# The first batch by pieces of two token tiles, all scores on eight 64 by 32 tiles, and TensorE in program order

**Chip, cores, metric.** One core of one Trainium2 chip. The metric is the device time of one execution in microseconds (us), median over runs. The kernel before takes 174.58 us (174.41 to 174.96, 3 runs).

## The reference

Attention over 4 batches, 8 heads, 768 tokens, head size 64, with a local window of 96 keys, 8 global keys and a distance bias; its output goes through a layer that multiplies by sines and cosines of a projection, mixes tokens with two 768 by 768 matrices, and applies a channel matrix.

```python
scores = scale * q @ k^T + bias            # bias = -slope[head] * distance
scores = where(is_global | is_local, scores, -1e9)
x = (softmax(scores) @ v) as [batch, token, 512]
theta = x @ w_theta
y = w_tok_r @ (x * cos(theta)) + w_tok_i @ (x * sin(theta))
u = x + y
out = u + max(u @ w_ch, 0)
```

## The kernel before

It works in stages that overlap between batches: *scores* and exponentials, *values*, transposes of x (xT), *theta* (projection, sines, products), *mix* (the token matrices, 72 matmuls of 512 columns a batch), transposes of u (uT), *chan* (the channel matrix), store. A head part, in program order, does the attention of batch 1. From then on the mixes of one batch ("main") are woven with the attention of the next ("side"), and a scheduler may reorder each engine.

The scores need the keys of tile jt and, for the next query tile, the last 96 of them with the 8 global keys in front. The kernel keeps a copy of the keys for that (kG):

```python
def kglob(b, p):
    kG = ...                                   # [128, 4, 128]
    nc.vector.tensor_copy(out=kG, in_=kT[:, T:5*T] ...)
    nc.vector.tensor_copy(out=kG[:, :, 0:NG], in_=kT[:, None, 0:NG] ...)

def score_mms(b, p, c):                        # one chunk: two key tiles, two heads
    for j in range(2):
        jt = 2 * c + j
        for part in range(2 if jt + 1 < NT else 1):
            for hh in range(2):
                R = slice(D * hh, D * (hh + 1))
                lhsT = kG[R, jt - 1, :] if part and jt else kT[R, own]
                nc.tensor.matmul(pb[:, hh, o:o + T], lhsT=lhsT, rhs=qT[R, (own, nxt)[part]], ...)

# preparation of a head pair: VectorE copies (qkn), TensorE transposes, copies qT (VectorE), kT (ScalarE)
# (cut) the weave of batch 1's main part; load_all_v(2) is its first side step
side[:0] = [(0, lambda: load_all_v(2))]        # fill of a column of ones on VectorE, then a DMA from GpSimd
weave(main, side, 0.3 if b == 0 else 0.0, 0.9)
```

The softmax here doesn't subtract the row's maximum and nothing guards it: scores larger than these inputs give would overflow.

## Time and profile before

| | before |
|---|---|
| time | 174.58 us |
| span of the profiled run | 172.6 us |
| TensorE / VectorE / ScalarE busy | 159.9 / 128.5 / 99.1 us |
| score matmuls, key copies | 352, 32 |
| instruction fetches for TensorE (queue q8) | 11 |

How to read: in the lines of profiles PE is TensorE, PEld its weight loads, DVE VectorE, ACT ScalarE, POOL GpSimd and SPq SyncE's queue; L12 is line 12 of that kernel's own source. Busy time of TensorE joins overlapping matmuls, so 93% busy isn't a full engine. The most useful ruler here turned out to be another one: the start of the n-th mix weight load, which is the same piece of work in every variant. Before, the 24th stands at 40.0 us, the first of batch 2 at 80.0, of batch 3 at 113.7, of batch 4 at 147.6, and the last of these loads (of 288) at 165.5.

### The profile page before, as it was taken

Reading aid. Unit: us, or ns where it says so; the run is one execution under the profiler, and the core shown is the slowest. Engines: PE = TensorE matmul, PEld = TensorE weight load, DVE = VectorE, ACT = ScalarE, POOL = GpSimd, SP = SyncE. Lnnn points to the kernel's source line nnn. Section 1 sums busy time; section 2 is a strip of 40 time slices with the busy share of each in tenths; the row PEclk is TensorE's granted clock in tenths of the full one; section 3 lists DMA queues with packets and bytes.
Section 4 is the critical chain, followed back from the end, with each engine's and each line's share of the span. In section 5 each row is a group of like instructions: output and inputs, shape, how many; then the busy total and the mean of one; then the engine's idle time right before and its main releaser. Section 6 shows DMA issues by size and latency. Waiting matters only on the chain.

```text
span 172.6 us, 3652 instructions
## 1 busy us (share of the span) xinstructions
PE 159.9 (93%) x1482; PEld 83.5 (48%) x1482; DVE 128.5 (74%) x288; ACT 99.1 (57%) x124; POOL 37.9 (22%) x45
## 2 busy tenths in 40 slices
PE   6479979999999999999999998999999989999991
PEld 1245655455756566544455463444554634444440
DVE  7678965678999999999587588597786837724443
ACT  2479676999497595489834740979348308500010
POOL 8974355005272010099300000000000000000000
PEclk9999999999999999999999999999999999999998
DMA  5999999999999999879999997787138571323335
GB/s 146 192 193 178 210 208 209 204 204 171 160 204 175 166 155 128 132 97 154 210 141 80 224 158 165 138 152 226 30 76 113 135 171 40 142 41 102 100 93 182
DMA packets 75088, 25.92 MB, mean 150 GB/s; under 512 B 63168, under 2 KB 72128, under 8 KB 75072
## 3 DMA queue, kind: packets, MB, share of 16 engines
q0 software_dynamic: 45680, 12.45, 78.4%
q1 hardware_dynamic: 28976, 12.72, 36.6%
q10 hardware_dynamic: 416, 0.52, 0.9%
q8 instruction: 11, 0.18, 0.4%
q14 instruction: 5, 0.04, 0.1%
HBM read 25.69 MB, written 6.29 MB: 185 GB/s over the span
## 4 chain that ended last, share of the span: by engine, by line
PE 59%; DVE 21%; ACT 10%; DMA 6%; issue 1%; SPq 0%; DVEq 0%; ACTq 0%
PE ps L409 29%; PE ps L434 10%; PE pb L389 5%; PE pb L295 4%; PE pb L352 4%; DVE x_sb L362 4%; ACT etab L142 3%; PE ps L389 3%; ACT e L302 3%; DMA qk<-in_k_dram 3%; DVE kG L218 2%; DVE e L312 2%; ACT cs L395 2%; DMA kT<-qk 2%; DMA xT<-x_sb 2%; PE ps L244 2%
## 5 line engine op out<-in xcount | busy, mean ns | idle before, releaser
L409 PE MATMUL ps<-zri,w_tokT 128*128 128x512 bf16 x288 | 70.6, 380 | 0.3 <-DVE o_sb L440 0.2
L302 ACT ACTIVATE e<-pb 128x1024 bf16<-128x1024 f32 (+1 forms) x48 | 43.6, 958 | 23.1 <-PE pb L295 22.9
L409 PEld LDWEIGHTS <-w_tokT 128*128 128x128 bf16 x288 | 26.1, 98 | 29.0 <-issue 1.0
L414 DVE TENSOR_TENSOR u<-x_sb,ps 128x512 bf16<-128x512 bf16 x24 | 16.4, 682 | 14.6 <-PE ps L409 14.6
L434 PE MATMUL ps<-w_ch_bf,uT 128*128 128x512 bf16 x96 | 24.2, 379 | 0.0
L398 DVE TENSOR_TENSOR zri<-x_sb,cs 128x512 bf16<-128x512 bf16 x48 | 17.9, 418 | 8.0 <-ACT cs L395 7.8
L440 DVE SCALAR_TENSOR_TENSOR o_sb<-ps,u 128x512 f32<-128x512 f32 (+1 forms) x25 | 16.5, 662 | 3.1 <-PE ps L434 3.1
L395 ACT ACTIVATE cs<-pb,halfpi 128x1024 bf16<-128x1024 f32 x8 | 8.9, 1116 | 15.7 <-PE pb L389 15.7
L312 DVE TENSOR_TENSOR e<-e,etab 128x1024 bf16<-128x1024 bf16 (+1 forms) x24 | 14.7, 615 | 3.4 <-ACT e L302 3.4
L389 PE MATMUL pb<-w_theta_bf,xT 128*128 128x512 bf16 x64 | 15.2, 379 | 1.0 <-DMA xT<-x_sb 1.0
L295 PE MATMUL pb<-qT,kT 64*128 64x128 bf16 x224 | 15.6, 219 | 0.6 <-DVE qT L211 0.3
L295 PEld LDWEIGHTS <-kT 64*128 64x128 bf16 x224 | 9.0, 94 | 14.1 <-issue 12.5
L389 PEld LDWEIGHTS <-xT 128*128 128x128 bf16 x96 | 9.0, 98 | 12.0 <-DMA xT<-x_sb 2.4
L428 ACT COPY uT<-ps 128x512 bf16<-128x512 bf16 x7 | 4.1, 587 | 18.6 <-PE ps L427 18.6
L352 PEld LDWEIGHTS <-e 128*128 128x128 bf16 x352 | 12.7, 97 | 3.3 <-issue 1.5
L434 PEld LDWEIGHTS <-uT 128*128 128x128 bf16 x96 | 8.9, 98 | 10.0 <-ACT uT L428 0.3
L295 PE MATMUL pb<-qT,kG 64*128 64x128 bf16 x128 | 11.7, 217 | 1.2 <-DVE kG L220 1.2
L88 POOL DMA_DIRECT2D vn<-in_v_dram x5 | 9.7, 1930 | 12.2 <-DVE vn L68 10.6
L362 DVE TENSOR_TENSOR x_sb<-pb,rec 128x768 bf16<-128x768 f32 x12 | 11.4, 949 | 0.3
L315 DVE TENSOR_TENSOR e<-e,etab 128x1024 bf16<-128x1024 bf16 x12 | 8.2, 684 | 2.8 <-ACT e L302 2.8
L352 PE MATMUL pb<-vn,e 128*128 128x65 bf16 x168 | 9.6, 193 | 0.3 <-DVE x_sb L362 0.3
L82 POOL DMA_DIRECT2D qk<-in_q_dram x8 | 7.4, 920 | 8.8 <-DVE qkn L229 5.0
(74 smaller groups left out, 203.0 us busy)
## 6 DMA issues: line engine op xcount, KB each, us to landing
out_dram<-o_sb SPq DMA_DIRECT2D x23, 256.0 KB, 2.4
vn<-in_v_dram POOLq DMA_DIRECT2D x3, 768.0 KB, 22.7
qk<-in_q_dram POOLq DMA_DIRECT2D x2, 768.0 KB, 21.0
qk<-in_k_dram POOLq DMA_DIRECT2D x2, 768.0 KB, 23.6
w_nat<-in_moe_w_tok_r_dram POOLq DMA_DIRECT2D x3, 384.0 KB, 13.7
w_nat<-in_moe_w_tok_i_dram POOLq DMA_DIRECT2D x3, 384.0 KB, 14.6
vn<-in_v_dram POOLq DMA_DIRECT2D x2, 384.0 KB, 8.9
qk<-in_q_dram POOLq DMA_DIRECT2D x8, 96.0 KB, 9.7
```

The source lines that it names most:

```text
L295: nc.tensor.matmul(pb[:, hh, o:o + T], lhsT=lhsT, rhs=qT[R, (own, nxt)[part]], start=bool(b), stop=bool(b) or (jt == NT - 1 or (j == 1 and ...
L302: ins = nc.scalar.activation(e_c, pb[:, :, 0:n], AF.Exp, scale=scale).ins
L312: nc.vector.tensor_mul(e_c, e_c, tab[:, :, s0:s0 + n // T].rearrange("p a s n -> p a (s n)"))
L352: nc.tensor.matmul(o, lhsT=l_, rhs=r_, start=(i_ == 0), stop=(i_ == len(mms) - 1))
L362: nc.vector.tensor_mul(xv, po4[:, :, :, 0:D], rec.to_broadcast([T, n, NT, D]))
L389: nc.tensor.matmul(pb[j_] if last else pb[:, j_, :], lhsT=xT[:, dc, st(j_)], rhs=w_theta_bf[:, dc, :], start=(dc == 0), stop=(dc == NC - 1))
L395: nc.scalar.activation(o, p_, AF.Sin, **bias)
L398: nc.vector.tensor_mul(zri[b][:, i_, 2 * c + j_, :].rearrange("p (g d) -> p g d", g=NP), xb[:, :, 2 * c + j_, :], cs[:, i_, j_].rearrange( ...
L409: anchor["pe"] = nc.tensor.matmul(ps, lhsT=w_tokT[wi][:, st, tt * T:(tt + 1) * T], rhs=zri[b][:, wi, st, :], start=(st == 0 and wi == 0), ...
L414: anchor["dve"] = nc.vector.tensor_add(u_sb[b, tt].rearrange("p (g d) -> p g d", g=NP), x_sb[b][:, :, tt, :], ps.rearrange("p (g d) -> p g ...
L434: nc.tensor.matmul(ps_c, lhsT=uT[:, dc, :], rhs=w_ch_bf[:, dc, :], start=(dc == 0), stop=(dc == NC - 1))
L440: nc.vector.scalar_tensor_tensor(o_sb[:, cols], in0=ps_c[:, cols], scalar=0.0, in1=u[:, cols], op0=ALU.max, op1=ALU.add)
```

## The change

Its intent: no key copies on VectorE (a group of 32 keys is its own TensorE tile, so the global keys can take the place of the first group), an earlier start of theta in batch 1, and a TensorE order that puts two chunks into each visit to the small tiles. The weave of batch 1 starts at 0.1 instead of 0.3. The diff, cut to its core:

```diff
-    def kglob(b, p): ...                       # and all its calls
     def score_mms(b, p, c):
-            for part in range(2 if jt + 1 < NT else 1):
-                for hh in range(2):
-                    lhsT = kG[R, jt - 1, :] if part and jt else kT[R, own]
-                    nc.tensor.matmul(pb[:, hh, o:o + T], lhsT=lhsT, rhs=qT[R, (own, nxt)[part]], ...)
+            for g in range(T // GS):           # four groups of 32 keys
+                own, P = slice(jt * T + g * GS, jt * T + (g + 1) * GS), slice(g * GS, (g + 1) * GS)
+                parts = [(own, 0, 1), (slice(0, GS), 1, n)][:n] if g == 0 and jt else [(own, 0, n)]
+                for keys, a, z in parts:
+                    for hh in range(2):
+                        nc.tensor.matmul(pb[P, hh, ...], lhsT=kT[R, keys], rhs=qT[R, ...], ...)
 # head: values0 and xtrans0 by chunks of two token tiles; theta, its products and the
 # first 24 mixes follow chunk by chunk (cut, about 150 lines)
+    ordered.enter_context(tc.manual_schedule(engines={PE}))     # until the end of the last weave
-        weave(main, side, 0.3 if b == 0 else 0.0, 0.9)
+        weave(main, side, 0.1 if b == 0 else 0.0, 0.9)
```

## The prediction

> **What bounds the kernel now.** I read the page's busy line first, then a table of busy time by stretch (columns: stretch, its length, then busy time and instruction count of each engine, granted clock, DMA), then the chain of waits, then the groups, and last the single matmuls of one stretch of scores.
>
> ```profile
> PE 159.9 (93%) x1482; PEld 83.5 (48%) x1482; DVE 128.5 (74%) x288; ACT 99.1 (57%) x124; POOL 37.9 (22%) x45
> ...
> 16.00:28.00 12.00, 10.19 (x171) 6.72 (x170) 10.12 (x29) 9.52 (x12) 6.07 (x6) 1.00 1.18 209
> 28.00:37.00 9.00, 8.90 (x52) 4.15 (x50) 5.81 (x16) 7.43 (x10) 0.41 (x1) 1.00 1.26 205
> ...
> 44.00:56.00 12.00, 11.79 (x148) 7.17 (x145) 12.00 (x28) 8.71 (x11) 5.38 (x7) 1.00 2.02 182
> 56.00:72.00 16.00, 15.28 (x201) 9.55 (x200) 16.00 (x36) 9.50 (x13) 1.18 (x2) 1.00 2.16 150
> ```
>
> TensorE is 93% busy, but busy time joins overlapping matmuls, their latency included, so it hides slack. I counted it otherwise: from start to start, a 512-column matmul takes 0.216 us, a 128-column one 0.056, a 65-column one 0.030, and a pair of score matmuls 0.056. Summed over the matmuls of a stretch this gives the work; the rest is slack. All matmuls come to 145.4 us. Slack by stretch: 0 to 28 us 11.9; 28 to 44 us 0.9; 44 to 72 us 5.0; 72 to 141 us 5.3; after that 4.2, mostly the last store. So two places can give: the head, and the stretch at 44 to 72 us, where VectorE is busy all of the time and sets the pace.
>
> The chain of waits (start, length, what) says the same:
>
> ```profile
> 0.74 4.37 DMA qk<-in_k_dram
> ...
> 7.78 1.01 DVE kG L218
> 8.81 0.18 DVE kG L220
> 9.04 0.25 PE pb L295 x2
> 9.32 1.94 ACT e L302 x2
> ...
> 36.01 1.28 ACT L142
> 37.31 5.12 ACT etab L142 x8
> 42.43 0.47 ACT uT L428
> 42.90 0.70 ACT kT L251
> 43.62 0.29 DVE kG L218
> ```
>
> The key copy kG stands before the first exponential; at 36 to 42.4 us the table load and the eight bias tables on ScalarE hold up the preparation of the second batch; then VectorE leads until 61 us; from there TensorE leads.
>
> **What the Trainium skill says.** (1) "TensorEngine Tiling (Array Packing)", section Key Properties: tiles work independently, but a change of tiling mode drains TensorE. The trace agrees with the drain: between the last 512-column matmul and the first score there are 0.31 us of start-to-start time where 0.22 would do, and on the way back 0.15 where 0.06 would do; a visit to the score mode costs some 0.19 us. (2) "TensorE: Matmul & The Clock Gate", section Measured speedup vs the span model: packed tiles start some 4 ns apart, for row and column tiles alike. For two row tiles the trace agrees: two score matmuls of 0.216 us are over within 0.22. No run yet shows column tiles. (3) The tiling page, section Restrictions: column tiling turns off the fast weight load. A load of 128 columns shows as 94 ns here and hides behind matmuls; what a load of 32 columns costs, the trace does not show.
>
> ```profile
> 81.50 0.22 PE L295 MATMUL pb<-qT,kG 64*128 64x128 bf16 x2
> 81.55 0.22 PE L295 MATMUL pb<-qT,kT 64*128 64x128 bf16 x2
> 81.61 0.22 PE L295 MATMUL pb<-qT,kG 64*128 64x128 bf16 x2
> 81.66 0.22 PE L295 MATMUL pb<-qT,kT 64*128 64x128 bf16 x2
> 81.72 0.22 PE L295 MATMUL pb<-qT,kG 64*128 64x128 bf16 x2
> 81.87 1.25 PE L409 MATMUL ps<-zri,w_tokT 128*128 128x512 bf16 x5
> ```
>
> **Part 1, scores on 64 by 32 tiles.** Before, a pair of heads took 22 score matmuls, 352 in all. Now chunks of two key tiles take 18, 20 and 18, so 56 a pair of heads and 896 in all: TensorE goes from 1482 to 1482 + 544 - 1 (one warm-up less) = 2025. The columns that each tile streams are the same: 256 a key tile, two matmuls at 0.056 = 0.112 us before, one of 256 (estimated 0.109 from 256/512 of 0.216) now. With eight tiles at 4 ns each, TensorE breaks even in steady flow. But matmuls start in order: in the first group of 32 keys the global keys need a second load and a second matmul, and groups 2 to 4 wait behind it, so a visit ends about 0.06 + 0.02 us later than before: 0.08 x 18 to 24 visits = +1.4 to +1.9 us, most of it in the TensorE-led part. In return the program order puts two chunks in every visit. The table by stretch shows visits split before: 54 changes of mode after 44 us, where 18 undivided visits make 36. (54 - 36) x 0.095 = -1.7 us. The two cancel.
>
> **Part 2, no key copies.** These groups go altogether:
>
> ```profile
> L218 DVE COPY kG<-kT 128x512 bf16<-128x512 bf16 x16 | 6.2, 388 | 1.3 <-DMA kT<-qk 0.7 <-ACT kT L211 0.5
> L220 DVE COPY kG<-kT 128x32 bf16<-128x32 bf16 x16 | 2.9, 179 | 0.2
> ```
>
> That is 9.1 us of VectorE. It counts only where VectorE leads: 1.2 us ahead of the first exponential, and about 2.2 us (four pairs at some 0.55) between 43 and 51 us. After 72 us it is hidden behind TensorE.
>
> **Part 3, the head in pieces.** New VectorE work: 12 divisions of 256 columns in place of 8 of 384 (estimate 12 x 0.54 against 8 x 0.68, +1.0), two copies taken over from ScalarE (+1.2). Net VectorE about -6.5, so near 122 us busy and 265 instructions. The dates: inputs land at 5.1 as before; cast 5.2 to 6.1, transposes to 6.6, copies to 7.5, scores to 8.0, so the first exponential is at 8.0 instead of 9.3. Then it slows: heads 2 and 3 land only at 8.3 to 8.9 (issue at 1.35 and 2.18 plus 7 us), so their cast cannot come forward. From there on TensorE, in order, costs about 1.0 us a chunk (bias 0.43, visit 0.19, scores 0.3) plus turns and values, 14 to 15 us for the rest; ScalarE's own sum is 8 x 0.93 + 4 x 0.72 + 3 x 0.70 = 12.4. The last exponential then ends at about 23.5 instead of 25.3, and theta starts at about 23.5 instead of 28.0. Not all of these 4.5 us is won: 1.7 us of values and transposes and 0.7 of weight transposes now come later, and in the strict order VectorE (24 to 37 us: divisions, copies, four products of 0.4 us each of three chunks) makes the first mixes wait some 2 us. By hand I arrive at 24 mix matmuls at 39 us, where the kernel before has 20 and one weight tile more. Gain on TensorE: 0 to 1.5 us. But ScalarE ends its sines some 2 us earlier, so the bias tables end near 40.5 and the second batch's preparation starts earlier.
>
> **Part 4, TensorE in program order.** No cost of its own; it removes the scheduler's filling of gaps. I allow 0 to +2 us.
>
> **Sum.** Head -0.8; 40 to 72 us: VectorE 2.2 us lighter and started 2 us earlier, limited by the 5.0 us of slack of which drains keep about 2.5: -2.3; after 72 us -0.3 (merged visits, no key copy in the chain at 106 us, against the 0.08 a visit); stalls of the fixed order +0.7. Together -2.7 from 174.58: **171.8 us**.
>
> **Rivals.** (a) The weight loads of 32 columns do not overlap. At some 27 ns each (an estimate: a 65-column matmul with its load is spaced 30 ns in the trace), 20 loads are 0.54 us a chunk instead of 0.22: +0.3 x 36 chunks where TensorE leads = +11 us, so 183 to 185. For it: the skill's word on fast load. Against: row tiles overlap down to 3 or 4 ns in the trace. (b) The fixed order stalls: scores wait for a free buffer, and TensorE, which before went to other work, stands still. Chunk pairs come some 2 us apart and two exponentials take 1.94, so it is tight; 18 pairs at 0.2 us = +3.6, so 176. (c) The head gains fully: if the divisions and products flow without the 2 us wait, mixes start near 30 us and the whole lead of 3 to 4.5 us stays: 168 to 169.
>
> **Range and chances.** The middle case is 171.8; (b) and a part of (a) give the upper end, 175.8, and (c) the lower, 168.5. The border for faster is 171.1, just below my middle. Faster 0.36, within 2% 0.54, slower 0.10 (that is (a)).
>
> **What would show it.** Matmuls 2025; kG gone; score matmuls of eight tiles starting within some 30 ns; a two-chunk visit at 0.6 to 0.7 us; first exponential near 8.0; last near 23.5; first sine near 25.5; bias tables ending near 40.5; VectorE near 122 us. Wrong would be: score spacing near 27 ns a matmul; waits of TensorE of over 0.2 us before scores in the later batches; or a dense TensorE from 24 us on, with no wait for the products.

## More of the kernel before

In batches 2 to 4 the transposes of x, u and some q and k are DMAs issued from SyncE, which also issues the stores: one queue, in order.

One line of the profile that the prediction did not look at will matter, TensorE's instruction fetches among the DMA queues (packets, MB, share):

```profile
q8 instruction: 11, 0.18, 0.4%
```

## The result, and the profile after

The changed kernel takes **183.06 us** median (181.22 to 184.04, 4 runs); before, in the same rounds, 174.77. The ratio is 1.0425 (95% interval 1.0324 to 1.0526): slower. A ratio is the mean time of one kernel's fast runs over that of the other's fast runs of the same rounds, so not quite the ratio of the medians. The profiled run is one marked slow (184.04 us, over 1.5% above the fastest); its mean TensorE clock, 0.991, lies between those of the runs marked fast (0.986, 0.987, 0.999). So what is read from it alone counts for that run only; the long copy and the theta stages below show in fast profiles of variants too (e1, e7).

The page of the changed kernel (busy times; then the span in 40 slices; then TensorE's fetches; then the scores):

```profile
PE 160.2 (88%) x1996; PEld 86.1 (47%) x2025; DVE 126.7 (70%) x265; ACT 97.6 (54%) x119; POOL 38.2 (21%) x45
...
PEclk9999999999699999999999999999999999999999
...
q8 instruction: 16, 0.26, 0.7%
...
L286 PE MATMUL pb<-qT,kT 64*32 64x256 bf16 (+1 forms) x896 | 17.4, 257 | 5.1 <-ACT e L294 2.3
```

The counts are as predicted (2025 weight loads; 29 matmul records are missing). TensorE has no more to do, yet the span is 9.4 us longer. The clock is down in one slice, at 45 to 50 us. And there are 16 fetches instead of 11.

A visit of two chunks to the small tiles, from the sequence of TensorE's work in batch 2:

```profile
87.30 0.38 PE L423 MATMUL ps<-zri,w_tokT 128*128 128x512 bf16 x1
87.61 0.63 PE L286 MATMUL pb<-qT,kT 64*32 64x256 bf16 x38
88.17 0.39 PE L423 MATMUL ps<-zri,w_tokT 128*128 128x512 bf16 x1
```

38 matmuls in 0.56 us from the first to the next mix; the same visit before took 0.55. The eight tiles of a group start 3.3 ns apart, and a load of 64 by 32 lasts 88 to 93 ns and hides. So the tiles themselves are what the prediction said.

Where the time went, by the start of the n-th mix weight load (us). The last two columns are the *theta stages*, from the last mix of one batch to the first of the next, which wait for the last xT:

| kernel | 24th | first of batch 2 | of 3 | of 4 | last | stage before 3 | stage before 4 |
|---|---|---|---|---|---|---|---|
| before | 40.0 | 80.0 | 113.7 | 147.6 | 165.5 | 8.7 | 8.6 |
| changed | 38.8 | 86.3 | 121.2 | 157.0 | 174.9 | 9.7 | 9.8 |

The head is 1.2 us ahead. The next 48 mixes, beside batch 2's attention, lose 7.5 us. The two theta stages lose 1.0 and 1.2. The mixes of batches 2 and 3 lose 0.2 and 0.7, those of batch 4 nothing.

The waits of the first loss, in the changed kernel's timeline (start, length, engine, work, idle time before and releaser):

```profile
41.14 0.10 DVE L68 MEMSET vn<- 128x48 bf16 x1
...
42.09 2.27 POOL L88 DMA_DIRECT2D vn<-in_v_dram  x1 [13.44 <-DVE qkn L221]
42.16 2.62 DVE L221 COPY qkn<-qk 128x768 bf16<-128x768 bf16 x3 [0.74 <-DMA qk<-in_k_dram]
...
44.71 0.94 DVE L241 COPY qT<-ps 128x768 bf16<-128x768 bf16 x1
...
45.70 0.49 PE L168 MATMUL ps<-ident,w_nat 128*128 128x128 bf16 x6 [1.95 <-DVE qT L241]
```

and the same in the kernel before, from the timelines of GpSimd and of VectorE:

```profile
39.05 2.21 POOL L88 DMA_DIRECT2D vn<-in_v_dram  x1 [10.64 <-DVE vn L68]
```

```profile
41.28 1.16 DVE L229 COPY qkn<-qk 128x768 bf16<-128x768 bf16 x4
42.35 0.95 DVE L249 COPY qT<-ps 128x768 bf16<-128x768 bf16 x1
```

Before, the fill of ones came at 38.1 us, so GpSimd issued the V load from 39.05 to 41.26 and the four copies of q and k ran undisturbed, 0.35 us each. After, the fill comes at 41.1, and GpSimd issues from 42.09 to 44.36. The new head makes it late: with the old weave start it still comes at 40.4 (e2 and h2 below). What the early weave start does is to bring the copies onto the issue; in e2 and h2 they begin at 44.4 and 44.2, after it. Here, of the three copies beside it, one lasts 2.08 us (42.44 to 44.52). It ends 0.16 us after the issue; in the fast profiles of e1, e7 and h1 a copy of 2.1 us ends 0.15 to 0.17 us after it. The Trainium skill, "SBUF — State Buffer", section Who interferes with whom, says that VectorE and GpSimd share a pair of ports under an exclusive lock, that a VectorE copy can take it, and that whichever comes second blocks fully. This trace agrees. The copy holds up qT, and TensorE, in its fixed order, stands at 43.7 to 45.7 us.

### The profile page after: what moved, and what is told of

The parts are those of the page before. It is cut to its first block, busy times and chain, and to the rows that moved or that the text cites.

```text
span 182.0 us, 4682 instructions
## 1 busy us (share of the span) xinstructions
PE 160.2 (88%) x1996; PEld 86.1 (47%) x2025; DVE 126.7 (70%) x265; ACT 97.6 (54%) x119; POOL 38.2 (21%) x45
## 4 chain that ended last, share of the span: by engine, by line
PE 56%; DMA 21%; ACT 10%; POOL 5%; DVE 4%; issue 3%; DVEq 0%; POOLq 0%
PE ps L423 27%; DMA qk<-in_k_dram 11%; PE ps L448 10%; DMA w_nat<-in_moe_w_tok_r_dram 7%; ACT e L294 5%; PE pb L392 4%; PE pb L341 4%; PE pb L286 4%; DMA xT<-x_sb 3%; PE ps L236 2%; POOL qk L73 2%; PE ps L392 2%; POOL vn L88 2%; DVE qkn L221 2%; ACT cs L400 1%
## 5 line engine op out<-in xcount | busy, mean ns | idle before, releaser
L423 PE MATMUL ps<-zri,w_tokT 128*128 128x512 bf16 x269 | 66.6, 382 | 2.9 <-issue 1.5
L448 PE MATMUL ps<-w_ch_bf,uT 128*128 128x512 bf16 x91 | 23.3, 379 | 0.4 <-issue 0.2
L286 PE MATMUL pb<-qT,kT 64*32 64x256 bf16 (+1 forms) x896 | 17.4, 257 | 5.1 <-ACT e L294 2.3
L400 ACT ACTIVATE cs<-pb,halfpi 128x1024 bf16<-128x1024 f32 x9 | 10.0, 1116 | 21.3 <-PE pb L392 20.5
L392 PE MATMUL pb<-w_theta_bf,xT 128*128 128x512 bf16 x70 | 17.1, 380 | 3.1 <-DMA xT<-x_sb 3.0
L286 PEld LDWEIGHTS <-kT 64*32 64x32 bf16 x896 | 10.8, 92 | 17.4 <-issue 13.3
L243 ACT COPY kT<-ps 128x768 bf16<-128x768 bf16 x8 | 6.4, 799 | 10.7 <-PE ps L236 10.7
L341 PEld LDWEIGHTS <-e 128*128 128x128 bf16 x264 | 9.6, 97 | 3.6 <-issue 1.4
L400 ACT ACTIVATE cs<-pb 128x1024 bf16<-128x1024 f32 x9 | 9.2, 1022 | 0.0
```

The lines of the kernel that those rows point to most:

```text
L286: nc.tensor.matmul(pb[P, hh, (2 * j + a) * T:(2 * j + z) * T], lhsT=kT[R, keys], rhs=qT[R, (jt + a) * T:(jt + z) * T], start=bool(b), stop ...
L341: nc.tensor.matmul(o, lhsT=l_, rhs=r_, start=(i_ == 0), stop=(i_ == len(mms) - 1))
L392: nc.tensor.matmul(pb[j_] if last else pb[:, j_, :], lhsT=xT_sb[b][:, dc, st(j_)], rhs=w_theta_bf[:, dc, :], start=(dc == 0), stop=(dc == ...
L400: nc.scalar.activation(o, p_, AF.Sin, **bias)
L423: anchor["pe"] = nc.tensor.matmul(ps, lhsT=w_tokT[wi][:, st, tt * T:(tt + 1) * T], rhs=zri[b][:, wi, st, :], start=(st == 0 and wi == 0), ...
L448: nc.tensor.matmul(ps_c, lhsT=uT[:, dc, :], rhs=w_ch_bf[:, dc, :], start=(dc == 0), stop=(dc == NC - 1))
```

## The experiments

"Before" in the same rounds was 174.67 to 174.80 throughout. Ratios are against it.

### One part at a time

**e1_sched_pe**: the changed kernel without the fixed order.

```diff
-    ordered.enter_context(tc.manual_schedule(engines={PE}))
```

> The changed kernel, but after the head TensorE's order is again left to the scheduler. Theory A (the fixed order makes TensorE stand behind prepared work of the second batch whose inputs have just landed and whose VectorE copies are late, and later behind the transposed copies of x): the stalls of some 6 us at 40 to 60 us and of 3 us in later batches go, 171 to 175 us. Theory B (the head in pieces leaves its VectorE work to the first batch's main part): little changes, 180 to 183 us.

178.39 us, 1.0200 (1.0143 to 1.0258). The fixed order costs some half of the loss.

**e2_late_side**: the changed kernel with the weave start of before.

```diff
-        weave(main, side, 0.1 if b == 0 else 0.0, 0.9)
+        weave(main, side, 0.3 if b == 0 else 0.0, 0.9)
```

> The changed kernel with the side work of the first batch starting at 0.3 of the main work, as before, instead of 0.1; the order stays fixed. Theory A with the early start as its main part: the 2.1 us wait at 43.5 us and the half-clock matmuls after it go, 176 to 179 us. If the fixed order is at fault whatever the start: 181 to 183 us. If it is the tiles or the head: 182 to 184 us.

186.45 us, 1.0623. A miss, and a lesson: the stall at 43 us is gone (36th mix at 43.2 us instead of 49.6), but batch 2's preparation now starts at 44.4 instead of 41.0, and more is lost afterwards (72nd mix at 80.5, against 78.1).

**e3_tiles_alone**: the kernel before with the eight tiles and without the key copies, nothing else.

```diff
-        kglob(b, p)                            # and the other calls
-    lhsT = kG[R, jt - 1, :] if part and jt else kT[R, own]     # 22 score matmuls a head pair
+    for g in range(T // GS): ...                               # 56 on 64 by 32 tiles
```

> The kernel before with only its scores on eight 64 by 32 tiles and without the key copies. From the changed kernel's trace, where a visit of two chunks takes 0.56 us as it did before: no loss on TensorE and some VectorE time given back, 171.5 to 174 us. If the tiles cost time that the spacing of matmuls does not show (changes of mode, 544 more instructions): 177 to 183 us.

177.84 us, 1.0172 (1.0126 to 1.0217): a clear miss. Less work on VectorE, the same on TensorE, and 3.1 us more. Milestones: 39.8, 80.8, 115.4, 150.8, 168.7. So +0.8 by the first mix of batch 2, and then theta stages of 9.4 and 9.6 us instead of 8.7 and 8.6.

**e4_order_alone**: the kernel before with TensorE in program order after the head.

```diff
+    ordered.enter_context(tc.manual_schedule(engines={PE}))
```

> The kernel before with only TensorE's order fixed to the program's after the head. Theory A: stalls in the first batch's main part and before the theta matmuls of later batches, 177 to 182 us. Theory B: no change, 174 to 176 us.

179.12 us, 1.0238 (1.0193 to 1.0283). The same first 24 mixes (40.4 us), then the first mix of batch 2 at 84.1 instead of 80.0; after that 0.6 us more go in the mixes of batch 3 (25.9 us from first to last, 25.3 before) and none in the theta stages (8.7 and 8.6). The waits of TensorE's matmuls from 40 to 72 us (us in total, times, longest), this kernel's first lines:

```profile
PE ps L244 <- DVE w_tokT L169: 2.0, 2, 1.7
PE pb L352 <- ACT e L302: 1.4, 2, 0.9
PE ps L244 <- DVE qkn L229: 0.7, 2, 0.5
```

and the kernel before, where these are all that are listed:

```profile
PE ps L244 <- DVE qkn L229: 0.3, 1, 0.3
PE pb L352 <- DVE x_sb L362: 0.3, 1, 0.3
```

So of the 5.9 us that e4's whole list holds, 2.7 are transposes of q and k behind VectorE's copies, 1.2 wait for ScalarE's copies and 2.0 for exponentials. In this stretch VectorE is nearly always busy (15.5 of 16 us from 40 to 56) and serves TensorE in an order of its own; a TensorE held to one order stands at every copy that is late.

**e6_tiles_and_order**: tiles and order in the kernel before, so the changed kernel without its head. 

```diff
     (e3's edit)
+    ordered.enter_context(tc.manual_schedule(engines={PE}))
```

> The kernel before with the 64 by 32 tiles and the fixed order, its head left alone: the changed kernel without its new head. If the three parts simply add (tiles alone +3.1 us, order alone +4.4): about 182 us. If the loss of the tiles comes only from the scheduler, which may take the small matmuls for long ones and so place the other work badly: with the order fixed there is no scheduler on TensorE, so about 178 to 179 us, as the order alone.

180.66 us, 1.0350. The parts nearly add (1.0172 x 1.0238 = 1.0414, and 1.0350 is measured); the changed kernel's 1.0425 is 0.7% above this one, with the head that was to gain, but the intervals (1.0324 to 1.0526 and 1.0319 to 1.0380) overlap.

**e7_order_later**: the changed kernel with the order fixed only from batch 2's main part on.

```diff
+        if b == 1:
             ordered.enter_context(tc.manual_schedule(engines={PE}))
```

> The changed kernel with the order fixed only from the second batch's own main part on; the first batch's main part, where VectorE is full, is left to the scheduler. If the fixed order costs only there (the trace of the order alone has its whole loss by 72 us): 178 to 179 us, like the changed kernel without the fixed order. If it costs in every batch: 181 to 183 us.

178.45 us, 1.0209: the same as with no fixed order (1.0200). The cost of the order, as far as the total shows it, lies in the main part of batch 1.

### Is it the stores in SyncE's queue?

In e3 the last xT of a batch stands in SyncE's queue behind other transposes and stores. A first guess was to take the stores out of that queue.

**e8_tiles_stores_on_gpsimd**, **e9_before_stores_on_gpsimd**: e3 and the kernel before with most stores issued from GpSimd.

```diff
-            (nc.scalar if i_ else nc.sync).dma_start(
+            (nc.scalar if i_ else nc.gpsimd if 0 < b < B - 1 or (b == 0 and tt >= 3) else nc.sync).dma_start(
```

> The kernel before with the 64 by 32 tiles, and the output stores of the first three batches issued by GpSimd instead of SyncE. Theory C: of the tiles' loss some 1.7 us stand at the theta matmuls of the third and fourth batch, which wait for the transposed copies of x, and those stand in SyncE's queue behind other transposes of 1.2 us and stores of 0.5 us each; with the stores out of that queue 175 to 176.5 us. If the queue is not the cause: 177.5 to 178.5 us, as the tiles alone.

> The kernel before with only the stores of the first three batches issued by GpSimd. Theory C: its two waits of 0.7 us for x at the theta matmuls shrink, 173 to 174.3 us. Otherwise 174.5 to 176 us.

180.17 us (1.0342) and 180.94 us (one of four runs marked fast, 177.22, so no ratio). Both worse, and confounded: GpSimd's stores then stood behind another wait on that engine. This settles nothing about the queue, only that this remedy is none.

### What lengthens the transposes

In the kernels with the tiles and no padding, one or two DMA transposes just ahead of the last xT take 1.7 to 2.8 us instead of 1.2. (Lengths here are the time that a transpose holds SyncE's queue; it lands later.) SyncE's queue before batch 4's theta (start, length), in the kernel before and in e3:

```profile
137.24 1.22 SPq L423 DMA_TRANSPOSE uT<-u  x1
138.55 1.24 SPq L366 DMA_TRANSPOSE xT<-x_sb  x1
```

```profile
139.50 2.11 SPq L415 DMA_TRANSPOSE uT<-u  x1
141.70 1.24 SPq L358 DMA_TRANSPOSE xT<-x_sb  x1
```

In the trace's DMA records each long transpose has a 16,384-byte transfer of the instruction queue q8 within it, or just at its start:

```text
kernel   long transpose (start, us)   fetch at
e3       qT  99.14  2.46              99.45
e3       uT 139.50  2.11             139.98
changed  qT 104.6   2.77             105.13
changed  uT 145.5   2.34             145.47
before   xT  90.66  2.32              91.28   (not on the path that sets the end)
before   (none near 137 to 139)      142.32   (after the last xT)
```

This holds over all 20 profiles: outside e8 and e9, none of the 539 transposes without a fetch in them lasts over 1.35 us; of the 141 with one, in all profiles, 80 last over 1.45, up to 2.77. So a fetch can lengthen a transpose but doesn't always, and it isn't the only thing that can: in e8 and e9, with stores on GpSimd, 5 of 60 last 1.56 to 2.14 us without one.

The Trainium skill, "Advanced Engine Details and Errata", section ISA Cache, gives a line of the instruction cache as 16 KB, 256 instructions. The records agree: 16,384 bytes, and about one for every 256 of TensorE's instructions, a weight load and a matmul counted apart. The tiles add 544 matmuls and as many loads, hence 16 fetches. That gives theory F: **a fetch of the longer instruction stream lands on a transpose ahead of the last xT**; its rival G: the tiles are slower by themselves. The two part under padding: idle matmuls of 8 columns at the start do no work, but move all later instructions in the stream and so the fetches in time.

```diff
     warm(6)
+    pad = ps_small([T, 512], FP)               # read by nothing
+    for _ in range(48):                        # 20 in f2
+        nc.tensor.matmul(pad[:, 0:8], lhsT=zero[:, 0:T], rhs=zero[:, 0:8], start=True, stop=True)
```

**f1_tiles_pad48** (e3 with 48), **f2_before_pad20**, **f3_sched_pad48** (e1 with 48), **f4_before_pad48**:

> The kernel before with the eight tiles and no key copies (177.84 us in its own run) plus 48 matmuls of 8 columns right after the warm-up, on zeros, into a PSUM tile that nothing reads. They do no work; they move every later TensorE instruction 48 matmuls on in the instruction stream, so that the 16,384-byte instruction fetches fall elsewhere: by the trace of the tiles alone at about 96.7 and 136.3 us in place of 99.5 and 140.0. Theory F (the tiles' cost is a fetch of TensorE's longer instruction stream that lands on a transposing DMA just ahead of the last xT of a batch, in the queue of SyncE): the qT transpose at 99 us takes 1.2 to 1.3 us in place of 2.46, the uT transpose at 139.5 takes 1.2 in place of 2.11, the theta stage of batch 4 shrinks by about 0.9 us and that of batch 3 by up to 0.7; 175.9 to 177.2 us. Rival G (the tiles are slower by themselves, or the longer stream costs wherever its fetches fall): 177.4 to 178.4 us, and the padding's own 48 matmuls at the start (about 0.5 us or less beside a wait for the first x tiles) only add.

> The kernel before with 20 such idle matmuls after the warm-up. Its last fetch moves from 142.3 us, after the last xT of batch 4, to about 137.5 us, onto the uT transpose at 137.24 that stands ahead of it. Theory F: that transpose takes about 2 us in place of 1.22, the theta stage of batch 4 begins its last step some 0.8 us later; 175.3 to 176.2 us, with no tile in the kernel. Rival G: 174.5 to 175.0 us, the same as before.

> The changed kernel without the fixed order of TensorE (178.39 us in its own run) plus the 48 idle matmuls: by its trace the fetches then fall at about 98.2 and 137.6 us in place of 101.0 and 140.9, off the qT transpose at 100.4 and the uT transpose at 140.9. Theory F: 176.4 to 177.8 us, the two transposes at 1.2 to 1.3 us. Rival G: 178.0 to 179.0 us.

> The control for the padding: the kernel before with 48 idle matmuls. Its fetches then fall at about 108.9, 126.2 and 135.5 us, between the transposes of the last theta stage. Theory F and rival G both: 174.5 to 175.3 us; if it is 175.5 or more, the padding itself costs and the other three have to be read against this one.

| kernel | time | ratio | stage before 3 | stage before 4 | fetches met in these stages |
|---|---|---|---|---|---|
| before | 174.7 | 1 | 8.7 | 8.6 | none that counts |
| f2 (before, 20) | 175.93 | 1.0067 | 8.7 | 9.4 | 138.51, last xT |
| f4 (before, 48) | 175.44 | 1.0049 | 8.9 | 8.7 | none; see text |
| e3 | 177.84 | 1.0172 | 9.4 | 9.6 | 99.45 qT, 139.98 uT |
| f1 (e3, 48) | 178.08 | 1.0197 | 10.1 | 8.7 | 96.52 xT, 105.00 uT |
| e1 | 178.39 | 1.0200 | 9.5 | 9.4 | 100.87 qT, 140.87 uT |
| f3 (e1, 48) | 177.54 | 1.0172 | 9.6 | 8.7 | 99.06 kT, 106.30 uT |

The times of f2 and f3 fell into the ranges of theory F. f2 is the cleanest: no tile in the kernel, and the last stage is 0.7 us longer as a fetch now meets the last xT:

```profile
137.29 1.22 SPq L423 DMA_TRANSPOSE uT<-u  x1
138.60 1.93 SPq L366 DMA_TRANSPOSE xT<-x_sb  x1
```

In f1 and f3 the last stage goes back to 8.7, with all the tiles still there. The totals are another matter. f1 missed its expectation of 175.9 to 177.2: the padding took the fetch off batch 4's transposes and put two on batch 3's, and the stretch from the 24th mix to batch 2 took 0.9 us more. With seven fetches between 80 and 150 us, and a queue that in those stages is seldom empty, some are met in any phase. f4 was to be the control, and it is 0.14 us above its range: up to the first mix of batch 3 it is level with the kernel before (within 0.1 us), then it loses 0.7 us with a fetch at 123.99 us during the uT transposes. So the padding itself costs nothing visible, and even the kernel before is 0.5 to 0.7% luckier in its fetches than these two neighbours. Theory F holds for the theta stages, with 0.7 to 1 us in this table for a fetch that meets a transpose on the path. It does not account for the 0.8 us that e3 loses before batch 2, nor for the mixes of batches 2 and 3. From first to last these take 25.2 and 25.8 us in e3, e1, f1 and f3 alike, wherever the fetches fall, against 24.9 and 25.3 before. So these 0.7 us look like rival G's, the tiles by themselves.

### Where the head's gain went

The head is ahead by 1.2 us and ends up behind. **h1_head_only_start10**: the new head, with its tiles for batch 1 only, before the old rest (key copies, no fixed order), weave start 0.1. **h2_head_only_start30**: the same with 0.3. **h3_tiles_sched_start30**: e1 with 0.3.

```diff
-    ordered.enter_context(tc.manual_schedule(engines={PE}))    # h1, h2, h3
+            if b:                              # h1, h2: batches 2 to 4 as before
+                ... lhsT = kG[R, jt - 1, :] if part and jt else kT[R, own] ...
+                continue
-        weave(main, side, 0.1 if b == 0 else 0.0, 0.9)
+        weave(main, side, 0.3 if b == 0 else 0.0, 0.9)         # h2, h3
```

> The head of the changed kernel (tiles for the scores of the first batch only) in front of the kernel before: for batches 2 to 4 the 64 by 128 key blocks and their copies are back, TensorE is not held to the program's order, the weave start stays at 0.1. The head gains 1.2 us by the 24th mix. If the tiles of batches 2 to 4 with their extra instruction fetches are what costs 3 us, this kernel is about 3 us below the one without the fixed order (178.39): 174 to 176 us, and its theta stages of batches 3 and 4 take 8.6 to 8.8 us again. If the head itself loses in the first batch's main part what it gained (the earlier weave start), it is 175 to 176. A rival by which the head changes nothing later gives 173.3 to 173.8.

> The same with the weave start of the kernel before, 0.3. If the head's gain was spent by starting the second batch's preparation too early, beside the work that VectorE is late with, this keeps it: 173.2 to 174.2 us, faster than the kernel before (174.7). If the preparation is the chain that ends last, it is slower than the start at 0.1, by 0.5 to 2 us.

> The changed kernel without the fixed order and with the weave start at 0.3: the same comparison with the tiles in all batches. Against 178.39 us with the start at 0.1: 176.9 to 177.9 if the early start is what spends the head's gain; 178.9 to 180.5 if the late one costs.

177.93 us (1.0175), 180.28 (1.0305), 182.03 (1.0402). All three missed, on the slow side (h2 and h3 in the direction of their second branch). What they tell: without the extra instructions of batches 2 to 4 (h1, h2) the theta stages ahead of batches 3 and 4 are back at 8.6 to 8.7 us, as theory F has it; the one ahead of batch 2 takes 10.1 and 11.3 us (8.1 before). But h1's 24th mix at 38.1 us is followed by the first of batch 2 at 82.0: 43.9 us for what takes 40.0 before. And the later start of the weave is worse each time, as in e2. In the changed kernel and in h1 the chain that ends last goes back from batch 2's attention to the landing of k; in the kernel before it runs through the bias tables. K is issued at 21.9 us and lands 19.4 us later, at 41.3, in the kernel before; at 42.1 in the changed one and 41.6 in h1. A head that is done sooner waits for the same transfer.

That is not all. The stretches from the 24th mix to the first of batch 2, in the kernel before and in h1 (stretch, length, busy time and count of PE, PEld, DVE, ACT, POOL, clock, DMA):

```profile
40.04:80.04 40.00, 39.06 (x427) 23.03 (x426) 39.31 (x91) 29.12 (x39) 14.21 (x17) 1.00 1.94 153
38.10:82.00 43.90, 40.25 (x438) 23.97 (x444) 42.25 (x94) 29.73 (x41) 15.53 (x18) 1.00 1.83 148
```

VectorE is busy for 98% and 96% of them. Up to its own 24th mix the new head (h1) has done 2.3 us less of VectorE's work (27.4 against 29.7), and 2.9 us more stand after it, 1.75 of them one long copy. As far as these counts show, the head is finished sooner in part by leaving work to the engine that then leads. No run tests this by itself.

**e5_channel_weights_later**: the changed kernel with the load of the channel weights issued after batch 2's q and k.

```diff
-        nc.gpsimd.dma_start(out=w_ch_bf, ...)  # in load_w
     load_all_qk(1)
+    nc.gpsimd.dma_start(out=w_ch_bf, ...)
```

> The changed kernel, fixed order and all, with the load of the channel weights issued after the loads of the second batch's q and k, which in the changed kernel landed at 42.1 us, just as the fixed order asked for their transposes. If the stall of TensorE at 43.5 us (2 us) is the late landing, it goes and the time is 180.5 to 182 us; if it is VectorE, slowed by GpSimd's issue of the V load beside it and by its own backlog, the stall stays in some form: 182.5 to 184 us.

179.83 us, 1.0280 (1.0238 to 1.0322): 3.2 us less than the changed kernel by the medians, 2.5 by the ratios, and better than either expectation. K lands at 39.5. But the longest q and k copy is now 0.43 us, so two things went together: k came earlier, and the copies were over before the V load's issue.

**g1_vload_early** takes them apart: the changed kernel with only the V load (and its fill) moved to the end of the head.

```diff
+    load_all_v(2)
     for p in range(NP):
         bias_table(p)
-            side[:0] = [(0, lambda: load_all_v(2))]
```

> The changed kernel, fixed order and all, with the V load of batch 3 (and the fill of its column of ones) issued at the end of the head, before the bias tables, in place of as the first step of the weave. In the changed kernel GpSimd issues it from 42.09 to 44.36 us and one VectorE copy of q and k beside it takes 2.08 us in place of 0.35; in the kernel before it is issued at 39.05, ahead of those copies. If that copy is what the fixed order stalls on (TensorE waits 1.9 us at 43.5), the long copy goes and the time is 180 to 181.5 us. If the late landing of k at 42.1 us is the cause, 182.5 to 183.5.

180.41 us, 1.0313 (1.0284 to 1.0342), inside the range that was set for the long copy. K lands at 42.13 as in the changed kernel; the issue runs from 40.36, and its timelines have

```profile
42.15 1.10 DVE L221 COPY qkn<-qk 128x768 bf16<-128x768 bf16 x3 [1.53 <-DMA qk<-in_k_dram]
```

in place of 2.62 us. Against e5, the earlier k is worth 0.6 us at most, within the intervals. The clock goes with the copy here. Busy time in two stretches of 4 us (PE, PEld, DVE, ACT, POOL with counts, then the granted clock), the changed kernel and g1:

```profile
44.00:48.00 4.00, 1.95 (x27) 1.67 (x27) 4.00 (x9) 1.06 (x2) 0.36 (x1) 0.90 2.67 168
48.00:52.00 4.00, 3.78 (x29) 2.41 (x27) 2.66 (x5) 1.86 (x3) 3.17 (x4) 0.67 1.32 204
```

```profile
44.00:48.00 4.00, 3.43 (x44) 2.71 (x44) 4.00 (x10) 2.17 (x4) 0.70 (x1) 1.00 2.62 169
48.00:52.00 4.00, 3.46 (x86) 1.77 (x88) 3.97 (x6) 2.97 (x5) 3.98 (x6) 1.00 1.31 204
```

In this run the changed kernel's TensorE is half idle for 4 us and then runs at 0.67 of its clock; g1's keeps 1.00. So the long copy can be paid twice: by the stall, and by the clock after it. The copy isn't needed for that: in e2 and h2, without one, TensorE is busy for 2.2 and 2.6 us from 44 to 48 us, and the clock is 0.61 and 0.65 in the next 4. The only run of the changed kernel with a mean clock of 0.999 took 181.22 us, the others, at 0.986 to 0.991, 183.03 to 184.04. All five timed runs of g1 have a clock of 1.00. In e1 the same copy lasts 2.11 us, but there TensorE finds other work (2.8 us busy from 44 to 48) and the clock stays at 1.00.

**g2_head_only_loads_moved**: h1 with both moves, the one candidate left to beat both kernels.

> The head in front of the kernel before (177.93 us; tiles in the first batch only, no fixed order) with both load moves: the V load at the end of the head, and the channel weights after the loads of the second batch's q and k. If the long VectorE copy and the late landing are where the head's gain went, the first batch's main part (24th mix to the first mix of batch 2) takes 40 to 42 us in place of 43.9 and the kernel 174 to 176 us; at the low end it beats the kernel before (174.7). If the weave start or the new head's order of work is what costs, 177 to 178.

177.14 us, 1.0141 (1.0111 to 1.0171): at the low end of the second range, in which the weave start or the head's order of work is what costs. It keeps one copy of 2.09 us (41.33 to 43.42), as V's issue (40.85 to 43.25) still meets the copies, so it is no clean test. From the 24th mix to the first of batch 2 it takes 43.1 us, with VectorE busy for 42.3, though k has landed at 39.2. No version tried beats the kernel before.

## Why the prediction was wrong

It said 171.8 us (168.5 to 175.8) and gave slower a chance of 0.10. By its own steps:

**Part 1, "The two cancel"**: right on TensorE (0.56 us a visit against 0.55), and rival (a), loads that don't overlap, is refuted. Wrong in what it left out: 1088 more TensorE instructions are also five more instruction fetches, and in the theta stages a fetch that meets a DMA transpose ahead of the last xT costs 0.7 to 1 us. That is 1.6 of the 3.1 us that the tiles cost alone (e3, and f1 to f3). Another 0.7 us lie in the mixes of batches 2 and 3, whatever the padding. The 0.8 us before batch 2 stay open.

**Part 2, "about 2.2 us ... between 43 and 51 us"**: the copies went, but VectorE's busy time fell by 1.8 us to 126.7 instead of 122 (1.7 of the 4.7 us between are the long copy), and the stretch gained nothing: in e3, with no other part of the change, the first exponential of batch 2 ends at 49.8 us instead of 48.6. There the chain that ends last runs, from 42 to 57 us, through the landing of k (41.8), transposes, ScalarE's copies and exponentials, and hardly through VectorE. So, as far as that one chain shows, another as long stood beside the one that was made shorter; this was not tested.

**Part 3, head "-0.8"**: the dates were good. 24 mixes at 38.8 us (39 predicted), the last exponential at 23.9 (23.5). The first exponential starts at 9.2, not 8.0 (before: 9.3). The step that failed is "the second batch's preparation starts earlier": k lands at 42.1 us (before: 41.3), and the bias tables end at 41.6, not 40.5. Worse, the late fill and the weave start of 0.1 put the V load's issue beside the copies (2.08 us for one; by g1 2.65 us of the time by the medians, 2.0 by the ratios). In place of -0.8, the head alone costs 3.1 us (h1), and VectorE's work that it leaves to the next stretch is in no term of the prediction. On top of the tiles it shows +0.3% (e1 against e3), on top of tiles and order +0.7% (the changed kernel against e6), neither clear of the intervals.

**Part 4, "I allow 0 to +2 us"**, taken as +0.7: this term was mis-sized by 3.7 us. Alone it costs 4.4 us (e4), nearly all of it in batch 1's main part (e4's first mix of batch 2 is 4.1 us late; e7). Rival (b) had the mechanism, but looked for it at scores that wait for a free buffer, in all 18 pairs of visits; such scores wait for 0.6 us in e4, and the longest waits are of transposes for VectorE's copies, in the one stretch where VectorE is busy for nearly all of the time. The prediction had marked that stretch as VectorE's and drew no conclusion for the order.

**The sum**: -2.7 predicted, +8.3 measured (+7.4 by the ratio). Each alone, the tiles cost 3.1 us, the order 4.4 and the head 3.1: 10.6 together, so the costs overlap in part, and no one split of the 8.3 is right. The sum's "-2.3" for 40 to 72 us is where most of the error lies: from the 24th mix to the first of batch 2 it is +7.5 us. Two smaller sums don't come out either: Part 3's terms make VectorE -6.9 us and not "about -6.5", and rival (b)'s 3.6 us in place of the 0.7 give 174.8 and not 176.

## What to carry to other kernels

Fixing an engine's order was cheap here only where that engine leads; beside another that is busy all of the time, leave it the freedom to fill, or check each wait of the fixed order against that engine's own order. Work that is finished sooner gains nothing ahead of a transfer that lands at a fixed time, or if it leaves more to the engine that leads next, so find what the next stage really starts on before counting it. And when an operation is cut into many small instructions, count the fetches of the longer stream too, and look in the DMA records for what they meet.

## What the Trainium skill lacked or had wrong

- "DMA: Bandwidth & Descriptors" says nothing of a DMA transpose beside an instruction fetch. Here a transpose of 1.2 us can take 1.7 to 2.8 us when a 16,384-byte fetch falls into it (f2: 1.93 instead of 1.24, only by 20 idle matmuls earlier in the stream).
- "Advanced Engine Details and Errata", ISA Cache, has the size of a line right. That the refill goes by a DMA queue stands in "Runtime: NRT & Kernel Launch", Instruction fetch mechanics, which calls its cost mostly hidden; no page has that it can delay other DMAs, as it does here in the theta stages (11 fetches before, 16 after).
- "TensorEngine Tiling (Array Packing)", Restrictions, warns that column tiling turns off the fast weight load. In the visit shown it cost nothing: 88 to 93 ns for a load of 64 by 32, hidden, and eight tiles 3.3 ns apart.
- "SBUF — State Buffer", Who interferes with whom, is right on the lock; its one figure for VectorE as the loser, 6.8 times slower, doesn't say beside what. Here a copy of 0.35 us took 2.08 beside an issue of 2.27 us.
- No page tells what a fixed order costs beside an engine that is always busy: 4.4 us of 174.7 here, in some 40 us of the kernel.
